# Banded attention and PReLU FFN: operands of the first layer laid out anew, and a planner that counts the order's rhythm

## The chip, the cores and the metric

The kernel runs on one core of a Trainium2 chip. The metric is the device time of one execution in microseconds (us). PE is the matmul engine (its weight loads have a row of their own, PEld), DVE the vector engine, ACT the scalar engine, POOL the GpSimd engine; SP issues the DMAs.

## The reference

Eight batches of eight heads, 576 positions, head size 64, all float32. The two parts run one after the other:

```
scores = q @ k.T / 8, kept where 0 <= i - j < 64
x = softmax(scores) @ v              # rearranged to 4608 tokens x 512
h = x @ w_in                         # 512 -> 2048
g = max(h, 0) + alpha * min(h, 0)    # alpha of each hidden column
out = g @ w_out                      # 2048 -> 512
```

## The kernel before

**Tiles and blocks.** The 4608 tokens are 36 tiles (`t`) of 128; four tiles are a block (`n`, 0 to 8). Matmuls run in fp32r: each value is a high part and a rest, and a product is hi times hi, hi times rest and rest times hi.

**First phase (to about 492 us).** Attention of a tile on PE is scores (`s.t`, line 548, 32 matmuls), then softmax on DVE, ACT and POOL, then the turning of the weights, then the values (`av`, line 604, one `av` for two tiles). A tile is turned either by PE (`tu.t`, line 588, 8 transposes; tiles listed in `PE_TURNED`, and ACT or DVE copies the result) or by DVE (`turn_by_vector`, lines 581 and 583, 16 transposes of 32x32 blocks). Blocks 0 and 1 take x through the first layer in cells (`h`, line 789, 12 matmuls of 512 columns; 16 cells a block). Blocks 2 to 8 use Strassen-like forms: a block has four groups (`d`), and a group has seven products (`p.n.d.i`, line 823) of 12 matmuls of 256 columns, in the order i = 1, 6, 5, 2, 7, 3, 4. Product 7 adds to a bank that DVE has combined from products 1, 6 and 5 (line 844). After the last products come PReLU on ACT and DVE (lines 837, 838) and a store of g to DRAM.

**Second phase (from about 492 us).** g is fetched again and made into seven forms a group (lines 934, 939, 940), which lie in ten slots used in turn (`yh_0` to `yh_9`); 252 products of 12 matmuls (`O`, line 967) follow, and the sums of the banks (line 975) and the writes of out.

**Order.** All instructions are written out in an order that `Program.order` plans: it knows a cost and a due time (`key`) for each step, and at each moment each engine takes the ready step that is due first. On PE products and attention steps compete by their keys. A group's product number `at` is due at `base + at * QUARTERS`; groups are `4 * CELL2` = 13.68 apart. Scores and values are due 0.03 ahead of the first product of a group, one score a group and one `av` every second group; the turning by PE falls due between the fifth and the sixth product. `convert_out` makes the weights of the second phase in four portions, one in each of the blocks 2, 4, 6 and 7 (`CONVERT_AT`).

**Addresses.** In a group's product the weights are the stationary operand and x the moving one. All weights lie at the same place modulo 512 bytes. From the sizes of the tiles (`step` 128 bytes, a row of x of 4160 bytes, gaps of 128 and 192 bytes) the distance from weights to x, modulo 256 bytes, is 128 for the products 1, 7 and 3 and 192 for 6, 5, 2 and 4 (5 and 6 read the buffers `s_forms`, sh and sl in the profile). In the cells of blocks 0 and 1 half of the matmuls have 128, half 192. In the second phase the forms are stationary and the weights move. Slots 0 to 3, 8 and 9 lie at 64 or 192 of the same count. Slots 4 to 7 can be shifted by steps of 64 bytes: usually by one step (64 or 192 again), but in the turns of the ring in `LEADS` (eight of them) slots 4, 5, 6 and 7 are shifted by 0, 1, 2 and 3 steps:

```
SHIFTS = [(x - 4, x - 4) if 4 <= x < 8 and turn in LEADS else (1, 1) for turn in range(26) for x in range(10)]
```

Of the kernel before, what the change touches and what calls it, by code (L numbers as in the profile page):

```python
# [23 lines left out]
BEGIN = 20.0  # L24
# [3 lines left out]
QUARTERS = 1.39  # L28
SINGLE = (0.5, 0.5, 9.5, 12.5, 28.0, 33.0, 35.0, 38.5)
HALVES = (11.0, 18.0)  # L30
EARLY_HALVES = 3
PACE = 3.8000000000000003
FIRST_TURN = 61.5
REBIASED = (0, 4, 5, 6, 8, 11, 12, 13, 14, 15)
PE_TURNED = (8, 14, 15, 17, 18, 19, 21, 22, 23, 25, 27, 28, 30, 31, 33, 34, 35)
CONVERT_AT = {2: 0, 4: 1, 6: 2, 7: 3}
# [5 lines left out]
CELL2 = 3.42  # L42
# [8 lines left out]
LEADS = (0, 1, 2, 3, 5, 8, 12, 17)  # L51
# [17 lines left out]
class Program:  # L69
# [25 lines left out]
    def order(self, fill):  # L95
# [10 lines left out]
        left, filling, warm_at = len(ops), False, None  # L106

# [38 lines left out]
        while left:  # L146
            for e in ENGINES:
# [17 lines left out]
                if e == "PE":  # L165
                    warm_at = now + COLD if warm_at is None else warm_at
                    o.busy *= 1 + (now < warm_at)
                if e == "POOL" and o.busy or e == "DVE" and o.paired:
                    o.busy += max(0.0, shared - now)
                    shared = now + o.busy  # L170
# [67 lines left out]
def banded_attention_then_prelu_ffn(  # L238
# [49 lines left out]
    def chunk_of(part, a):  # L288
        y, x = divmod(a, 2)
        return part[:, y, x * BT * P:(x + 1) * BT * P]  # L290

    def chunks_of(part, x, tiles):

        return part[:, :, x * BT * P:(x + 1) * BT * P].rearrange("p a (i q) -> p i a q", q=P)[:, tiles]

    def quarter_of(part, y, m):
        return part[:, y, :2 * BT * P].rearrange("p (x t) -> p x t", x=2)[:, :, m * 2 * P:(m + 1) * 2 * P]

    xs = [buffers_of_x(const, 0)]
# [6 lines left out]
    const.tile([P, 16], F32, name="rest")  # L306
# [359 lines left out]
    def quarter_parts(ts):  # L666

        n = ts[0] // BT
        for x in range(2):
            a21, a22 = (bank_of(V_BANK[x]).rearrange("p (i a) q -> p a i q", i=2)[:, a] for a in range(2))  # L670
            k = halves_of(V_BANK[x])
            hi, lo = (chunks_of(part, x, slice(2, BT))[:, :, 1] for part in xs[n % 2])
# [7 lines left out]
    def x_form(n, i):  # L680
# [4 lines left out]
        elif i in (5, 6):  # L685
# [3 lines left out]
        return ([quarter_of(part, y, m) for part in xs[slot]],  # L689
# [22 lines left out]
    def x_parts(ts, by=V_BANK):  # L712
# [4 lines left out]
        pieces = [([x], [chunks_of(part, x, slice(i, i + len(ts))) for part in xs[n % 2]],  # L717
# [27 lines left out]
    def attend_two(ts, begin, pace, before):  # L745
# [27 lines left out]
    def cell(n, f, key, m=None):  # L773
# [12 lines left out]
        def emit():  # L786
            for k, (w, v) in enumerate(((w_hi, xh), (w_hi, xl), (w_lo, xh))):
                for a in range(NP):
                    nc.tensor.matmul(h, w[KEPT + f][:, a * P:(a + 1) * P], chunk_of(v, a)[:, half], start=k == a == 0, stop=k == 2 and a == NP - 1, skip_group_check=True)
# [17 lines left out]
    def group(n, d, base):  # L807
# [6 lines left out]
        def product(at, i, bank, new):  # L814
# [3 lines left out]
            def emit():  # L818
# [46 lines left out]
    SHIFTS = [(x - 4, x - 4) if 4 <= x < 8 and turn in LEADS else (1, 1) for turn in range(26) for x in range(10)]  # L865
# [51 lines left out]
    def second(n):  # L917
# [4 lines left out]
        for d in range(DUOS):  # L922
# [10 lines left out]
            def both(name, to, a, b, op, reads, writes):  # L933
                add(name, "DVE", 0.61, lambda: nc.vector.tensor_tensor(out=to(), in0=a(), in1=b(), op=op), reads, writes)  # L934

            def parts(i, value, ks):
# [4 lines left out]
                    [*ks, *his], los)  # L941
# [64 lines left out]
    for n in range(NB):  # L1006
        step, off = (CELL, 0.5) if n < N0 else (CELL2, 0.01)
# [86 lines left out]
```

## Time and profile before

| | |
|---|---|
| three runs, us | median 846.36 (845.23 to 850.14) |
| profiled execution, us | 847.71 |
| its span, first to last instruction, us | 846.0 |
| granted TensorE clock, mean | 1.000 |
| PE, DVE, ACT, POOL busy, share of the span | 98%, 81%, 61%, 44% |

A profile shows one execution. Matmuls are pipelined: the busy time of one is longer than the time to the start of the next, so what a product takes is read from the starts of instructions in the timeline. There a line stands for several like instructions in a row ("x2"), and a product of 12 matmuls is six such lines, of which the rows below show the first. In the second phase a line holds four matmuls and a product three lines.

### The profile page before, as it was taken

The page shows a single profiled execution, that of the slowest core. Times are in us where ns is not written, and L with a number is a line of the kernel's source. Part 1 is how long each engine was busy: PE and PEld are TensorE (multiplying, and loading weights), DVE is VectorE, ACT ScalarE, POOL GpSimd, SP SyncE. Part 2 cuts the span into 40 slices and gives each one's busy share as a digit, 9 for nine tenths or more (in the row PEclk, how much of TensorE's full clock was granted, in tenths as well). Part 3 has the DMA queues.
Part 4 walks back from the last instruction along what each step waited for, and adds up shares of the span by engine and source line. Part 5 has one row for each costly group of instructions (what it writes and reads, how often), then busy time and mean ns, then how long its engine had stood idle before and what let it go on. Part 6 is the DMA issues. An engine that isn't in the chain of part 4 may idle for free.

```text
span 846.0 us, 23601 instructions
## 1 busy us (share of the span) xinstructions
PE 832.5 (98%) x8998; PEld 798.2 (94%) x8998; DVE 688.3 (81%) x1773; ACT 513.9 (61%) x1388; POOL 374.9 (44%) x368
## 2 busy tenths in 40 slices
PE   8999999999999999999999989999999999999998
PEld 8987788999999999999999989999999999999998
DVE  4888897879888888888875599979797887969794
ACT  6887757777778775697865664444443444444441
POOL 5899899989564661738557862000000000000000
PEclk9999999999999999999999999999999999999999
DMA  8886456445766743676574893537262543526341
GB/s 248 273 271 190 152 171 203 150 149 180 250 238 202 229 169 127 222 240 208 176 234 156 280 307 109 156 106 219 63 207 79 172 131 119 158 102 198 103 140 50
DMA packets 108880, 150.95 MB, mean 178 GB/s; under 512 B 10464, under 2 KB 69856, under 8 KB 108768
## 3 DMA queue, kind: packets, MB, share of 16 engines
q1 hardware_dynamic: 106416, 149.19, 55.1%
q8 instruction: 70, 1.15, 0.6%
q10 hardware_dynamic: 2352, 0.27, 0.2%
q14 instruction: 42, 0.34, 0.1%
HBM read 94.90 MB, written 54.53 MB: 177 GB/s over the span
## 4 chain that ended last, share of the span: by engine, by line
PE 68%; DVE 6%; ACT 2%; issue 2%; DMA 2%; SPq 0%; DVEq 0%; ACTq 0%
PE bank L967 39%; PE bank L823 24%; PE bank L604 2%; PE bank L548 2%; DVE cell L838 1%; DVE yl L940 1%; PE bank L588 1%; DVE bank L844 1%; DMA wo<-val 1%; ACT cell L837 1%; DVE g L934 1%; DMA raw<-w_out 1%; ACT r L851 0%; ACT w L564 0%; DVE pt L581 0%
## 5 line engine op out<-in xcount | busy, mean ns | idle before, releaser
L940 DVE TENSOR_TENSOR yl<-g,yh 128x512 fp32r<-128x512 f32 x216 | 149.5, 712 | 39.5 <-ACT yh L939 36.4
L939 ACT CAST yh<-g 128x512 fp32r<-128x512 f32 x216 | 125.1, 619 | 92.4 <-DVE g L934 64.9
L967 PE MATMUL bank<-wh,yl 128*128 128x256 f32 x1008 | 156.5, 277 | 2.4 <-DVE yl L940 2.3
L967 PE MATMUL bank<-wh,yh 128*128 128x256 f32 x1008 | 156.1, 277 | 1.0 <-DVE cell L838 1.0
L967 PE MATMUL bank<-wl,yh 128*128 128x256 f32 x1008 | 155.9, 277 | 0.0
L967 PEld LDWEIGHTS bank<-wh,yl 128*128 128x128 f32 x1008 | 133.6, 188 | 3.2 <-DVE yl L940 3.2
L967 PEld LDWEIGHTS bank<-wh,yh 128*128 128x128 f32 x1008 | 133.6, 188 | 1.2 <-DVE cell L838 1.2
L967 PEld LDWEIGHTS bank<-wl,yh 128*128 128x128 f32 x1008 | 133.6, 188 | 0.0
L564 ACT ACTIVATE w<-w,nm 128x128 f32<-128x128 f32 x288 | 112.4, 394 | 23.5 <-DVE nm L557 23.3
L838 DVE SCALAR_TENSOR_TENSOR cell<-bank,alphas,cell 128x256 f32<-128x256 f32 x224 | 96.0, 478 | 33.0 <-ACT cell L837 31.8
L823 PE MATMUL bank<-xh,wh 128*128 128x256 f32 x560 | 116.5, 290 | 3.8 <-DVE bank L844 2.4
L837 ACT ACTIVATE cell<-bank,alphas 128x256 f32<-128x256 f32 x224 | 91.5, 473 | 43.4 <-DVE bank L844 21.3
L823 PE MATMUL bank<-xl,wh 128*128 128x256 f32 x560 | 111.1, 280 | 0.0
L823 PE MATMUL bank<-xh,wl 128*128 128x256 f32 x560 | 111.0, 280 | 0.0
L573 POOL TENSOR_TENSOR w<-w,rc 128x512 f32<-128x512 f32 x72 | 76.1, 1074 | 53.3 <-DVE rc L569 39.9
L823 PEld LDWEIGHTS bank<-xh,wh 128*128 128x128 f32 x560 | 85.0, 188 | 10.0 <-DVE bank L844 4.8
L823 PEld LDWEIGHTS bank<-xh,wl 128*128 128x128 f32 x560 | 85.5, 188 | 0.0
L823 PEld LDWEIGHTS bank<-xl,wh 128*128 128x128 f32 x560 | 85.4, 188 | 0.0
L934 DVE TENSOR_TENSOR g<-g,g 128x512 f32<-128x512 f32 x108 | 77.0, 713 | 0.7
L844 DVE TENSOR_TENSOR bank<-bank,r 128x512 f32<-128x512 f32 x84 | 58.4, 695 | 23.2 <-PE bank L823 10.2
L557 DVE CUSTOM_DVE_ANT_0 w<-bank,masks 128x128 f32<-128x128 f32 x288 | 64.8, 285 | 10.3 <-PE bank L548 10.0
L939 ACT CAST yh<-diff 128x512 fp32r<-128x512 f32 x36 | 22.4, 623 | 76.3 <-DVE diff L934 56.2
(96 smaller groups left out, 1499.2 us busy)
## 6 DMA issues: line engine op xcount, KB each, us to landing
g<-g SPq DMA_DIRECT2D x144, 256.0 KB, 4.6
g<-cell SPq DMA_DIRECT2D x141, 256.0 KB, 3.1
out<-cell SPq DMA_DIRECT2D x36, 256.0 KB, 2.4
q<-qT SPq DMA_DIRECT2D x35, 256.0 KB, 4.3
raw<-w_out SPq DMA_DIRECT2D x16, 512.0 KB, 5.4
wl<-wo SPq DMA_DIRECT2D x28, 256.0 KB, 4.4
v<-vN SPq DMA_DIRECT2D x18, 384.0 KB, 5.3
k<-kT SPq DMA_DIRECT2D x17, 384.0 KB, 4.3
```

What stands on the lines that cost most here:

```text
L548: nc.tensor.matmul(bank_of(score_banks(t, a)[x])[us, 2 * a + h], q[r, a, h, us], kring[r, a, at + u:at + u + 2, h, :], start=True, stop=True)
L557: nc.vector.tensor_tensor_reduce(out=of_head(weights[t % 2], g), in0=bank_of(score_banks(t, g // NP)[x])[:, e].rearrange("p (b k) -> p b k ...
L564: nc.scalar.activation(w, w, AF.Exp, scale=-1.0, bias=least[t % 2][:, g:g + 1], accum_out=sums[:, t % 2, g, 0:1])
L573: nc.gpsimd.tensor_tensor(out=w, in0=w, in1=rc.unsqueeze(1).unsqueeze(3).broadcast_to(list(w.shape)), op=ALU.mult)
L823: nc.tensor.matmul(h, at_place(w, place)[:, c * P:(c + 1) * P], v[:, c], start=new and j == 0 and not done, stop=j == 1 and done == 5, ski ...
L837: add(f"sl.{n}.{d}.{m}.{x}.{j}", "ACT", 0.36, lambda h=h, g=g, f=f: nc.scalar.activation(g, h, AF.Copy, scale=slope[:, f:f + 1]), ["signs" ...
L838: add(f"la.{n}.{d}.{m}.{x}.{j}", "DVE", 0.43, lambda h=h, g=g, f=f: nc.vector.scalar_tensor_tensor(out=g, in0=h, scalar=sign[:, f:f + 1], ...
L844: add(f"{name}.{n}.{d}", "DVE", 0.6, lambda: nc.vector.tensor_tensor(out=to, in0=a, in1=b, op=ALU.add), reads, k_to)
L934: add(name, "DVE", 0.61, lambda: nc.vector.tensor_tensor(out=to(), in0=a(), in1=b(), op=op), reads, writes)
L939: add(f"ys.{u}.{i}.h", "ACT", 0.54, lambda: nc.scalar.copy(y_of(y_hi, x, hi), value()), [*ks, "right"], his)
L940: add(f"ys.{u}.{i}.l", "DVE", 0.61, lambda: nc.vector.tensor_tensor(out=y_of(y_lo, x, lo), in0=value(), in1=y_of(y_hi, x, hi).bitcast(F32) ...
L967: nc.tensor.matmul(banks[bank][:, h * EH:(h + 1) * EH], part[:, j * HW + h * P:j * HW + (h + 1) * P], w[k][:, j * EH:(j + 1) * EH], start= ...
```

## The change

It has these parts.

- **Layout of x.** The buffers of x lose their gaps, so that all lie 192 bytes from the weights (modulo 256). `s_forms` now holds products 5 and 7 in place of 5 and 6, and product 7's buffers stand after a gap that puts them at 128. So of the seven products only 7, the fifth of the order, lies at 128. The cells of blocks 0 and 1 are all at 192.
- **Due times.** Products are due every 1.362 (`STEP`); the sixth and seventh are due at the same time as the fifth (`VISIT`). Groups are 12.72 apart (`CELL2` = 3.18). Attention in blocks 2 to 8 is due 7 products earlier (`EARLIER`), and the turning by PE a whole group, or two, after the tile's pair begins (`TURNS`), so that all attention steps of a group are due 3.13 to 3.16 after its first product.
- **Costs in the planner.** A product costs 1.425 if it is a 7, 1.362 if only products have run since a 7, else 1.413; a change between products and anything else on PE costs 0.1. DVE passes of the second phase are counted as sharing a port with POOL (`paired`).
- **Tiles and portions.** Tiles 15, 19 and 23 are turned by DVE, no longer by PE. The first two portions of `convert_out` move from blocks 2 and 4 to 3 and 5. The starts of blocks 0 and 1 are shifted by 0.5 to 4.5.
- **Lead-in.** In the turns of `LEADS` (eight again, other ones) only slot 6 is shifted, by two steps, which is 128; the other slots stay at one step.

```diff
-BEGIN = 20.0
+BEGIN = 23.0
-QUARTERS = 1.39
-SINGLE = (0.5, 0.5, 9.5, 12.5, 28.0, 33.0, 35.0, 38.5)
-HALVES = (11.0, 18.0)
+SLOW, ENTRY, CHANGE = 1.413, 1.425, 0.1
+TURNS = (1.0, 2.0)
+HOLD = 0
+VISIT = 4.0
+EARLIER = 7.0
+SINGLE = (0.5, 0.5, 9.5, 11.5, 28.0, 30.5, 35.5, 37.5)
+HALVES = (12.0, 18.0)
-FIRST_TURN = 61.5
+FIRST_TURN = 57.0
-PE_TURNED = (8, 14, 15, 17, 18, 19, 21, 22, 23, 25, 27, 28, 30, 31, 33, 34, 35)
-CONVERT_AT = {2: 0, 4: 1, 6: 2, 7: 3}
+PE_TURNED = (8, 14, 17, 18, 21, 22, 25, 27, 28, 30, 31, 33, 34, 35)
+CONVERT_AT = {3: 0, 5: 1, 6: 2, 7: 3}
-CELL2 = 3.42
+CELL2 = 3.18
-LEADS = (0, 1, 2, 3, 5, 8, 12, 17)
+LEADS = (0, 1, 2, 3, 4, 5, 7, 9)
...
+        steady, lately = False, ("", 0.0)
...
+                if e == "PE":
+                    quarters, before = o.name[:2] == "p.", lately[0][:2] == "p."
+                    if quarters:
+                        steady = steady and before and now - lately[1] < 0.05
+                        entry = o.name[-1] == "7"
+                        o.busy = ENTRY if entry else STEP if steady else SLOW
+                        steady = steady or entry
+                    o.busy += CHANGE * (quarters != before)
+                    lately = o.name, now + o.busy
...
-    const.tile([P, 32], F32, name="step")
-
-    def buffers_of_x(pool, slot):
-
-        both = []
-        for x in "hl":
-            both.append(pool.tile([P, 2, 2 * BT * P + 16], F32R, name=f"x{x}_{slot}"))
-            if x == "h":
-                pool.tile([P, 32], F32, name=f"gap_{slot}")
-        return both
...
-    xs = [buffers_of_x(const, 0)]
+    const.tile([P, 48], F32, name="step")
+    xs = [[const.tile([P, NP, BT * P], F32R, name=f"x{x}_0") for x in "hl"]]
...
-    const.tile([P, 16], F32, name="rest")
+    const.tile([P, 48], F32, name="rest")
...
-    xs.append(buffers_of_x(odd, 1))
+    xs.append([odd.tile([P, NP, BT * P], F32R, name=f"x{x}_1") for x in "hl"])
+    s_forms = {5: [odd.tile([P, 2, 2 * P], F32R, name=f"s{x}_5") for x in "hl"]}
     odd.tile([P, 48], F32, name="gap")
-    s_forms = {i: [odd.tile([P, 2, 2 * P], F32R, name=f"s{x}_{i}") for x in "hl"] for i in (5, 6)}
+    s_forms[7] = [odd.tile([P, 2, 2 * P], F32R, name=f"s{x}_7") for x in "hl"]
...
-                turned_by_pe(t, V_BANK, begin + (0.5 + i) * pace)
+                turned_by_pe(t, V_BANK, begin + (TURNS[i] if t // BT >= N0 else 0.5 + i) * pace - 0.02)
...
-            add(f"p.{n}.{d}.{i}", "PE", QUARTERS, emit, [k for x in "hl" for place in places for k in w_keys_of(x, place[0], [place[1]])] + ks[0] + ks[1],
-                halves_of(bank), key=base + at * QUARTERS)
+            add(f"p.{n}.{d}.{i}", "PE", STEP, emit, [k for x in "hl" for place in places for k in w_keys_of(x, place[0], [place[1]])] + ks[0] + ks[1],
+                halves_of(bank), key=base + (at * STEP if at < 5 else VISIT * STEP - HOLD))
...
-    SHIFTS = [(x - 4, x - 4) if 4 <= x < 8 and turn in LEADS else (1, 1) for turn in range(26) for x in range(10)]
+    SHIFTS = [(2, 2) if x == 6 and turn in LEADS else (1, 1) for turn in range(26) for x in range(10)]
...
-        step, off = (CELL, 0.5) if n < N0 else (CELL2, 0.01)
+        step, off = (CELL, 0.5) if n < N0 else (CELL2, 0.01 + EARLIER * STEP / CELL2)
```

The rest of the diff adapts the views of x to its new layout and adds `paired=True` to the DVE passes of lines 934 and 940.

## Rows read from the trace of the kernel before

**Rows 1.** The page: busy time of each engine (part 1), the chain's lines (part 4).

```profile
PE 832.5 (98%) x8998; PEld 798.2 (94%) x8998; DVE 688.3 (81%) x1773; ACT 513.9 (61%) x1388; POOL 374.9 (44%) x368
...
PE bank L967 39%; PE bank L823 24%; PE bank L604 2%; PE bank L548 2%; DVE cell L838 1%; DVE yl L940 1%; PE bank L588 1%; DVE bank L844 1%; DMA wo<-val 1%; ACT cell L837 1%; DVE g L934 1%; DMA raw<-w_out 1%; ACT r L851 0%; ACT w L564 0%; DVE pt L581 0%
```

**Rows 2.** Windows: us, busy (instructions) PE PEld DVE ACT POOL, PEclk, DMA share, GB/s.

```profile
147.00:399.00 252.00, 249.79 (x3359) 241.81 (x3355) 213.78 (x731) 189.94 (x612) 164.03 (x158) 1.00 0.60 195
348.00:399.00 51.00, 50.52 (x697) 48.42 (x696) 44.82 (x153) 39.81 (x125) 31.36 (x27) 1.00 0.67 216
399.00:451.00 52.00, 51.45 (x615) 50.08 (x614) 39.19 (x108) 36.07 (x98) 33.92 (x30) 1.00 0.58 193
...
492.00:530.00 38.00, 34.64 (x290) 33.65 (x289) 37.58 (x48) 19.44 (x37) 16.89 (x11) 1.00 0.54 176
```

**Rows 3.** Timeline of PE, 238 to 251 us: start, us, what, xcount.

```profile
241.15 0.39 PE L823 MATMUL bank<-sh,wh 128*128 128x256 f32 x2
...
242.51 0.39 PE L823 MATMUL bank<-xh,wh 128*128 128x256 f32 x2
...
243.97 1.10 PE L548 MATMUL bank<-k,q 64*64 64x128 f32 x32
245.00 0.50 PE L823 MATMUL bank<-xh,wh 128*128 128x256 f32 x2
...
246.53 0.40 PE L823 MATMUL bank<-xh,wh 128*128 128x256 f32 x2
...
247.95 0.40 PE L823 MATMUL bank<-xh,wh 128*128 128x256 f32 x2
...
249.34 0.40 PE L823 MATMUL bank<-xh,wh 128*128 128x256 f32 x2
...
250.77 0.40 PE L823 MATMUL bank<-sh,wh 128*128 128x256 f32 x2
```

**Rows 4.** Timeline of PE, 366 to 372 us.

```profile
368.37 0.40 PE L823 MATMUL bank<-sh,wh 128*128 128x256 f32 x2
...
369.78 0.40 PE L823 MATMUL bank<-xh,wh 128*128 128x256 f32 x2
...
371.20 1.03 PE L588 MATMUL bank<-ident,w 128*128 128x128 f32 x8
371.99 0.37 PE L823 MATMUL bank<-xh,wh 128*128 128x256 f32 x1
```

**Rows 5.** Timeline of PE: the first and the last attention visit of the 49.

```profile
159.26 1.10 PE L548 MATMUL bank<-k,q 64*64 64x128 f32 x32
...
438.96 2.04 PE L604 MATMUL bank<-pt,v 64*64 64x128 f32 x96
```

**Rows 6.** Groups by line on DVE, 147 to 451 us: the 32x32 transposes.

```profile
L581 DVE STREAM_TRANSPOSE pt<-w 32x256 f32<-32x256 f32 x56 | 24.4, 435 | 1.5 <-POOL w L573 0.4
L583 DVE STREAM_TRANSPOSE pt<-w 32x128 f32<-32x128 f32 x56 | 17.0, 303 | 1.2
```

**Rows 7.** Waits, 147.04 to 492.25 us: us in total, times, longest.

```profile
PE bank L823 <- DVE bank L844: 2.4, 4, 1.0
...
PE bank L823 <- DVE cell L838: 1.0, 3, 0.5
```

**Rows 8.** Timeline of PE, 542 to 552 us, second phase.

```profile
544.15 0.64 PE L967 MATMUL bank<-wh,yh 128*128 128x256 f32 x4
...
547.00 0.64 PE L967 MATMUL bank<-wh,yh 128*128 128x256 f32 x4
...
548.43 0.63 PE L967 MATMUL bank<-wh,yh 128*128 128x256 f32 x4
...
549.84 0.62 PE L967 MATMUL bank<-wh,yh 128*128 128x256 f32 x4
```

**Rows 9.** Timeline of PE, 99 to 106 us: matmuls of 512 columns.

```profile
99.68 1.09 PE L789 MATMUL bank<-xh,wh 128*128 128x512 f32 x4
...
102.46 1.09 PE L789 MATMUL bank<-xh,wh 128*128 128x512 f32 x4
```

More of the change, by code (lines that the diff above doesn't have):

```diff
@@ L276, in banded_attention_then_prelu_ffn @@
     w_hi, w_lo = ([const.tile([P, 512], F32R, name=f"w{x}_{k}") for k in range(7 * DUOS)] for x in "hl")
-    const.tile([P, 32], F32, name="step")
-    def buffers_of_x(pool, slot):
-        both = []
-        for x in "hl":
-            both.append(pool.tile([P, 2, 2 * BT * P + 16], F32R, name=f"x{x}_{slot}"))
-            if x == "h":
-                pool.tile([P, 32], F32, name=f"gap_{slot}")
-        return both
[L288 to L297, printed above, removed]
-    xs = [buffers_of_x(const, 0)]
+    const.tile([P, 48], F32, name="step")
+    xs = [[const.tile([P, NP, BT * P], F32R, name=f"x{x}_0") for x in "hl"]]
     sums_of = [const.tile([P, 512], F32, name="r_0")]
@@ L671, in quarter_parts @@
             k = halves_of(V_BANK[x])
-            hi, lo = (chunks_of(part, x, slice(2, BT))[:, :, 1] for part in xs[n % 2])
+            hi, lo = (part.rearrange("p (a x) (i q) -> p x i a q", x=2, q=P)[:, x, 2:, 1] for part in xs[n % 2])
             his, los = (x_keys(part, 4 * (n % 2) + 2 + x, range(2, 4)) for part in ("xh", "xl"))
@@ L684, in x_form @@
             (y, m), slot = rows[i], n % 2
-        elif i in (5, 6):
+        elif i in s_forms:
             return s_forms[i], [[f"s{x}.{i}"] for x in "hl"]
@@ L688, in x_form @@
             (y, m), slot = (0, 1), (N0 + (i == 3)) % 2
-        return ([quarter_of(part, y, m) for part in xs[slot]],
+        return ([part[:, 2 * y:2 * y + 2, m * 2 * P:(m + 1) * 2 * P] for part in xs[slot]],
                 [[k for c in (2 * y, 2 * y + 1) for k in x_keys(part, 4 * slot + c, (2 * m, 2 * m + 1))] for part in ("xh", "xl")])
@@ L716, in x_parts @@
         copy, other, pass_ = (0.48, 0.6, 0.61) if len(ts) == 2 else (0.36, 0.34, 0.35)
-        pieces = [([x], [chunks_of(part, x, slice(i, i + len(ts))) for part in xs[n % 2]],
+        pieces = [([x], [part.rearrange("p (a x) (i q) -> p x i a q", x=2, q=P)[:, x, i:i + len(ts)] for part in xs[n % 2]],
                    bank_of(by[x]).rearrange("p (i a) q -> p i a q", i=2)[:, :len(ts)], halves_of(by[x])) for x in range(2)]
@@ L788, in emit @@
                 for a in range(NP):
-                    nc.tensor.matmul(h, w[KEPT + f][:, a * P:(a + 1) * P], chunk_of(v, a)[:, half], start=k == a == 0, stop=k == 2 and a == NP - 1, skip_group_check=True)
+                    nc.tensor.matmul(h, w[KEPT + f][:, a * P:(a + 1) * P], v[:, a, half], start=k == a == 0, stop=k == 2 and a == NP - 1, skip_group_check=True)
         tiles = range(BT) if m is None else range(m * BT // 2, (m + 1) * BT // 2)
@@ L933, in both @@
             def both(name, to, a, b, op, reads, writes):
-                add(name, "DVE", 0.61, lambda: nc.vector.tensor_tensor(out=to(), in0=a(), in1=b(), op=op), reads, writes)
+                add(name, "DVE", 0.61, lambda: nc.vector.tensor_tensor(out=to(), in0=a(), in1=b(), op=op), reads, writes, paired=True)
             def parts(i, value, ks):
@@ L940, in parts @@
                 add(f"ys.{u}.{i}.l", "DVE", 0.61, lambda: nc.vector.tensor_tensor(out=y_of(y_lo, x, lo), in0=value(), in1=y_of(y_hi, x, hi).bitcast(F32), op=ALU.subtract),
-                    [*ks, *his], los)
+                    [*ks, *his], los, paired=True)
             a11, a12, a21, a22 = (cell(q) for q in range(4))
@@ L1041, in banded_attention_then_prelu_ffn @@
     add("right", "POOL", 0.0, open_right, (), [*early_keys, "right"])
-    add("left", "POOL", 0.0, open_left, ["right"], [*odd_x, *staged[0], *staged[1], *(f"s{x}.{i}" for x in "hl" for i in (5, 6)), "left"])
+    add("left", "POOL", 0.0, open_left, ["right"], [*odd_x, *staged[0], *staged[1], *(f"s{x}.{i}" for x in "hl" for i in s_forms), "left"])
     for n in range(NB):
```

## Prediction

> **What bounds the kernel now.** I read the page first [rows 1]: PE is busy 98% of the span, and the chain that ended last lies for 39% on the products of the second phase and for 24% on those of the groups. DVE is next, at 81%. Then the windows, to see whether another engine is close in a stage [rows 2]. While groups and attention run together (147 to 451 us, two rows of the group) PE is all but always busy, and DVE has 213.78 + 39.19 = 253.0 of 304 us, 83%; its densest block is 348 to 399 with 44.82 of 51, 88%. Only between the phases, 492 to 530, does DVE fill its time (37.58 of 38) and PE stand still for some 3.4 us. So the first phase is as long as PE's list of work, and since a busy PE is not one at its peak, the question is how long each product takes from its start to the next start. That is what the timeline of PE shows.
>
> In [rows 3] the reader sees products 5 and 2 of a group, a visit of attention (scores), 7, 3, 4 and the next group's 1, with a product from the s buffers behind it. The starts are apart by 1.36 (5), 1.46 (2, with scores behind it), 1.03 (the scores), 1.53 (7, with scores ahead of it), 1.42 (3), 1.39 (4), 1.43 (1). Three prices follow. A product at distance 128 takes 1.42 to 1.43; I use 1.425. The first at 192 behind one at 128 takes 1.39, every further one 1.36. And a visit costs 0.10 on the product ahead of it and 0.10 on the one behind it. A fourth price is in [rows 4]: two products at 192 that follow a visit with no product at 128 between take 1.41 each. So a quick rhythm is entered by way of a product at 128, kept by products at 192, and lost at 128 and at many visits.
>
> **Rhythm of the products.** There are 28 groups (7 blocks of 4). Over 7 x 1.36, a group now spends 3 x 0.065 on 1, 7 and 3 and 2 x 0.03 on the products behind them: 0.255, in all 7.1 us. Afterwards only 7 is at 128: 0.065 + 0.03 = 0.095 a group, 2.7 us. By the keys attention comes 3.13 to 3.16 after a group's first product, between the third (due 2.72) and the fourth (4.09); so in the 24 groups with attention I expect a visit ahead of product 2, which then runs at 1.41: 24 x 0.05 = 1.2. If attention in fact falls ahead of 7, this is 0. I take 3.9 in place of 7.1: **-3.2** (bounds -4.4, and +3.2 if the quick rhythm isn't entered, below).
>
> **Visits.** In the timeline of 147 to 492 I count 49 visits, of which [rows 5] has the first and the last; 28 begin with scores or values, which make the product ahead of them longer, while one that begins with transposes costs it 0.01 (1.42 after 1.41 in [rows 4]). With one due time a group, a pair of tiles needs in its first group the turning of its first tile and the next pair's scores together, and in the second the scores and values, in one visit, or in two where the second tile is turned by PE (the values wait for the copies of its turned weights; meanwhile product 2 runs). With 7 such pairs and 4 others, 7 x 3 + 4 x 2 and one more at the start: 30 visits, some 18 of them with a price ahead. That saves 19 x 0.10 + 10 x 0.09: **-2.8** (bounds 0 and -4, the latter with a visit in each of the 24 groups).
>
> **Turning.** Three tiles fewer on PE, at 0.79 for eight transposes [rows 4]: **-2.4**. In exchange DVE gets 8 x 0.435 + 8 x 0.303 = 5.9 us a tile [rows 6], 17.7 us in all, and loses at most some copies of turned weights. This is hidden only while DVE has slack: 253.0 + 17.7 = 270.7 us in what would be 296 us is 91%, above the 88% of its densest block. Behind a late DVE stand the sums of line 844 that product 7 waits for, the PReLU passes that free a bank, and the next scores' minima. PE now waits 2.4 + 1.0 us for DVE there [rows 7], 1.0 of it in one wait. I let half of the 2.4 come once more: **+1.2** (bounds 0, as PE's visits give the sums more time, and +12, below).
>
> **Lead-in.** Of the second phase's slots 4 to 7, four products in a turn of `LEADS` take 549.84 - 544.15 = 5.69, which is 0.25 over 4 x 1.36; eight turns, 2.0 us [rows 8]. Slot 6, at 128, takes 1.43 there and the next 1.41. Afterwards only these two remain, 0.07 + 0.03 to 0.05, eight times 0.11: 0.9 us. **-1.1** (bounds -1.3 and 0, if leaving out slots 4 and 5 keeps the rhythm from returning).
>
> **What I cost at nothing.** The cells of blocks 0 and 1: 12 matmuls of 512 columns take 2.78 [rows 9]; at the quick rate of two products they would take 2.72, at 1.41 2.82, so with 29 whole cells the bounds are -1.7 and +1.2. The other starts of blocks 0 and 1 shift steps of a PE that has no idle time in that stage: -2 to +2. Between the phases the plan now knows that DVE and POOL share a port, which can reorder the forms and weights; PE's idle time of 3.4 us there bounds this: -3.4 to +3.4. The portions of `convert_out` that move, with 4 loads and 7 stores each on SP's queue, feed only the second phase, over 200 us later; the DMA engines are at 0.60 in 147 to 399 [rows 2], so there is room. The DVE work of those portions stays the same in sum. The layout adds no instruction.
>
> **Sum.** -3.2 - 2.8 - 2.4 + 1.2 - 1.1 = -8.3. The span of 846.0 becomes 837.7, and with the 1.7 that the profiled execution has outside it 839.4 in place of 847.7. That execution was 1.35 above the median of the three, 846.36, so the forecast of the median is 838.0 us.
>
> A rule of the Trainium skill speaks against the largest terms. TensorE: Matmul & The Clock Gate, section "Step-by-step: what each phase is for", says that TensorE reads weights and moving operand through two independent ports, so that loading the next weights takes no read bandwidth from the running matmul. Read strictly, where the operands lie would not matter, and of the sum only visits and turning would be left (the second rival). The trace disagrees: products of the same shape, back to back, take 1.36 or 1.43.
>
> **Rivals.** (1) *The quick rhythm isn't entered behind 7.* Then the six products at 192 stay at 1.41: 0.065 + 6 x 0.05 = 0.365 a group, 10.2 us against 7.1 now, +3.1 in place of -3.2: 844.3. For it: [rows 4], where the rhythm once lost stayed lost, and 7 now has a visit close ahead. Against: 4 behind 3 in [rows 3]. Chance 0.13.
> (2) *Addresses aren't the cause*, the two paces come from something that travels with the products' order: rhythm and lead-in give nothing, -2.8 - 2.4 + 1.2 = -4.0: 842.4. The rule of the Trainium skill named above would have it so. Against: the second phase, where the only thing that differs in the turns of `LEADS` is the shift [rows 8]. Chance 0.05.
> (3) *DVE becomes the bound*, the case on the other side. If it can't be filled beyond the 88% of its best block, 270.7 us of work need 308 us where PE would need 296: +12, 849.6. At the mean of 147 to 399, 213.78 / 252 = 85%, they need 319 us: 861. It decides at 89%: there the gain is gone. For it: DVE works in a fixed order and often stands behind ACT. Against: those waits shrink when DVE is the late one, and in 492 to 530 it was filled to 99% [rows 2]. Chance 0.12.
> (4) *More is won*: attention ahead of 7 (-1.2), cells at the quick rate (-1.7), half of the idle time between the phases (-1.7): 833.4. Chance 0.15.
>
> My forecast keeps 0.55. A change of 0.5%, 4.2 us, is about what a measurement of this kernel tells from none. Below 842.1 lie nearly all of the forecast's own cases (0.52), (4), half of (2) and a few of (1): 0.72. Above 850.6 lies about two thirds of (3) and a little else: 0.10. Between, 0.18. The range takes in (4) with the lower bounds of the small terms, 831, and (1), (2) and the near end of (3), 847; outside are the rest of (3) and several lower bounds at once.
>
> **What would show it.** Rhythm: in the timeline of a block such as the fifth, starts 1.36 apart for 4, 1, 6 and 5, and one of 1.39 behind 7; six at 1.41 would be rival 1. Visits: about 30 in the stretch of the groups, and a tu alone only ahead of product 2. Turning: 13 tiles of transposes on PE there; DVE at 90% in the windows, and PE's waits for lines 844 and 838 not far above 3.4 us; 10 us or more would be rival 3. Lead-in: in turns such as the eighth one product at 1.43, with 1.36 ahead of it. The first group should start near 147, the second phase near 485. The forecast is wrong if the scores aren't ready when due, so that visits scatter, if 7 waits for its DVE sums in most groups, or if the idle time between the phases grows by several us because the last portions and forms come no sooner than before.

## The result, and the profile after

The changed kernel takes 836.58 us (median of 4 runs, 836.05 to 837.52), the kernel before 848.25 beside it (4 runs, 845.23 to 851.24): a ratio of 0.9864, 95% interval 0.9821 to 0.9906. Over the longer series that went with the experiments the kernel before stood at 846.72 to 846.92, so the gain is 10.1 to 10.3 us rather than the 11.7 of this pair. The profiled execution of the changed kernel took 836.5 us with a span of 834.8, where before had 847.7 and 846.0: 11.2 us less span, and 8.3 were forecast.

The page of the changed kernel, busy time of each engine and the chain by line; lines 817 and 961 are what 823 and 967 were in [rows 1]:

```profile
PE 823.8 (99%) x8974; PEld 792.0 (95%) x8974; DVE 704.9 (84%) x1821; ACT 518.1 (62%) x1382; POOL 386.3 (46%) x368
...
PE bank L961 41%; PE bank L817 13%; DVE cell L832 1%; PE bank L598 1%; DVE bank L838 1%; PE bank L582 1%; DMA q<-qT 1%; PE bank L542 0%; ACT cell L831 0%; DVE w L551 0%; ACT w L558 0%; DVE pt L577 0%; DVE pt L575 0%; ACT r L845 0%; DVE xl L717 0%
```

PE's busy time fell by 8.7 us and DVE's rose by 16.6. The windows (columns as in [rows 2]) say where:

```profile
147.00:399.00 252.00, 247.48 (x3356) 239.64 (x3355) 233.70 (x790) 190.25 (x616) 168.56 (x160) 1.00 0.62 206
...
451.00:492.00 41.00, 40.15 (x343) 39.80 (x342) 30.15 (x54) 28.25 (x62) 35.53 (x28) 1.00 0.85 275
492.00:530.00 38.00, 38.00 (x331) 38.00 (x330) 33.27 (x50) 20.98 (x37) 19.41 (x8) 1.00 0.73 246
```

In 147 to 399 DVE is busy 233.70 of 252 us, 93%, where it had 85%, and PE has lost 2.3 us of busy time. In 492 to 530 PE is busy all the time, where 34.64 of 38 us were busy before. The two show the two halves of the story: the groups run with a fuller DVE, and the stretch between the phases has lost its idle time.

The timeline of PE over one group of block 4, of each product the first line (each stands for two of its twelve matmuls):

```profile
262.47 0.39 PE L817 MATMUL bank<-xh,wh 128*128 128x256 f32 x2
...
263.83 0.39 PE L817 MATMUL bank<-sh,wh 128*128 128x256 f32 x2
...
265.19 1.03 PE L582 MATMUL bank<-ident,w 128*128 128x128 f32 x8
266.16 1.10 PE L542 MATMUL bank<-k,q 64*64 64x128 f32 x32
267.19 0.50 PE L817 MATMUL bank<-xh,wh 128*128 128x256 f32 x2
...
268.68 0.40 PE L817 MATMUL bank<-sh,wh 128*128 128x256 f32 x2
...
270.11 0.40 PE L817 MATMUL bank<-xh,wh 128*128 128x256 f32 x2
...
271.50 0.39 PE L817 MATMUL bank<-xh,wh 128*128 128x256 f32 x2
...
272.86 0.39 PE L817 MATMUL bank<-xh,wh 128*128 128x256 f32 x2
```

Against [rows 3]: products 6 and 5 take 1.36 each, the turning and the scores now lie in one visit ahead of product 2, product 7 at 128 takes 1.43 (268.68 to 270.11), 3 behind it 1.39, and from 4 on it is 1.36.

**The sum by one walk.** For each kernel I walked along PE's matmuls from the first group's product to the end of the last product of the second phase. The 448 products are taken at 1.36 each, 609.28 us; what is above that is sorted by the steps from one matmul's start to the next. Steps of 113 to 119 ns are the rhythm. A first or last step of a product above 150 ns is the price of a visit; a last one above 260, or one in the middle above 150, is a wait. Two things the sorting mixes: a wait behind a visit, ahead of the next product, falls into attention's own time, and where the granted clock was at half behind a long wait (e3, e4 and e11) the slower steps, 1.4 to 2.1 us in each, fall into the waits. Columns: the stretch in us, number of visits, rhythm of the groups' products, price of visits, attention's own time (scores, values, turning), waits in the groups, waits in the second phase, and the rhythm and visits of the second phase. Each line adds up to its stretch within 0.02.

```
                     stretch visits rhythm price attention waits g waits 2nd 2nd
before                695.01   49    7.05  8.54   58.50     4.55    4.76     2.32
after                 684.16   32    4.74  6.68   55.21     6.73    0.16     1.36
e10 late fetch        690.63   32    4.08  6.70   55.21     8.53    5.78     1.04
e3 unpaired           694.52   32    4.08  6.66   55.21    10.06    7.98     1.26
e1 addresses back     684.52   32    8.23  5.99   55.03     4.48    0.16     1.34
e2 no entry           682.80   32    5.49  6.08   55.09     5.35    0.16     1.34
e5 turned by PE       691.13   35    4.64  7.20   57.69     9.06    1.82     1.43
e4 attention late     715.94   41    4.97  9.01   60.45    29.88    1.37     0.99
e6 no leads           695.61   32    3.73  6.61   55.22     7.08    0.22    13.47
e9 fourth behind      684.12   34    4.37  6.37   57.18     4.18    1.80     0.95
e8 layout alone       693.62   49    4.31  8.88   59.39     4.62    4.80     2.34
e11 before, fetch     698.29   49    7.01  8.41   58.60     5.84    6.57     2.59
e12 fetch + paired    690.92   49    6.91  8.28   58.60     3.92    1.70     2.24
e13 e2, sooner lead   684.09   32    4.83  6.50   55.08     7.24    0.27     0.90
```

Each line is one profiled execution. After, e2, e6 and e13 run the groups by the same plan and have 5.35 to 7.24 us of waits there, so less than 2 us in that column tells nothing. What lies ahead of the first group's product is left out: it was 145.8 to 148.5 us in ten of the fourteen profiles and 151.2 to 152.8 in the other four (e1, e4, e8, e11; last section).

From before to after the walk gives -2.31 in the rhythm, -1.86 in the price of visits, -3.29 in attention's time, +2.18 in the groups' waits, -4.60 in the second phase's waits, and -0.96 in its rhythm: -10.85, with -0.53 ahead of the stretch and +0.19 behind it the 11.2 of the span.

**Where the largest part came from.** Three products of the second phase now run among the last groups. The timeline of PE, first lines of the first such product and of the group's product behind it, and the fetch of g on SP's queue that it hangs on:

```profile
451.23 1.33 SPq L921 DMA_DIRECT2D g<-g  x3
```

```profile
462.28 0.63 PE L961 MATMUL bank<-wh,yh 128*128 128x256 f32 x4
...
463.69 0.41 PE L817 MATMUL bank<-sh,wh 128*128 128x256 f32 x2
```

The first fetch and the first product of the second phase in the kernel before:

```profile
480.95 1.38 SPq L927 DMA_DIRECT2D g<-g  x3
```

```profile
492.25 0.63 PE L967 MATMUL bank<-wh,yh 128*128 128x256 f32 x4
```

There the fetch came 29.7 us later, no product of the second phase ran until the last of the groups had been issued, and the first ones then stood waiting for their forms: 2.3 us for line 940 and 1.0 for line 838. The program issues the fetch of g `earliest=base - 45` ahead of the second phase as the plan dates it, and that date hangs on `CELL2`, which the change lowered from 3.42 to 3.18: 28 groups of 4 x 0.24 are 26.9 us, less the 3 by which `BEGIN` rose, so the second phase was dated 23.9 us sooner. So a constant of the groups' pace moved the fetch.

**Where it was given back.** PE's waits for lines 838 and 832 (844 and 838 before, [rows 7]), groups only; columns: us in total, times, longest:

```profile
PE bank L817 <- DVE bank L838: 4.7, 9, 0.9
PE bank L817 <- DVE cell L832: 0.6, 2, 0.5
```

5.3 us against 3.4. Six of the eleven, 3.1 us, have one form, as here in the timeline of PE in block 5: product 3, then 4.

```profile
333.64 0.39 PE L817 MATMUL bank<-xh,wh 128*128 128x256 f32 x2
...
335.63 0.50 PE L817 MATMUL bank<-xh,wh 128*128 128x256 f32 x2 [0.46 <-DVE bank L838]
```

Product 4 needs a bank that DVE adds up from what 7 left, and only 3 lies between. Along the timelines, a visit lay between 7 and 4 in 11 of the 28 groups before and lies there in none now; a visit stood right ahead of 7 in 21 groups and now stands there in 10. So DVE has less time for that sum; but in [rows 3] the three lie together too and PE doesn't wait, so the order alone doesn't make the wait. In five of the six DVE's two passes of line 832 (the PReLU) come shortly ahead of the late sum, in the one shown a pass of 1.41 us of `convert_out`.

### The profile page after: what moved, and what is told of

Its sections match the earlier page's. It is cut to its first block, busy times and chain, and to the rows that moved or that the text cites. A ratio compares the mean times of both kernels' runs of the same rounds, so it can differ in the third digit from the quotient of the medians.

```text
span 834.8 us, 23747 instructions
## 1 busy us (share of the span) xinstructions
PE 823.8 (99%) x8974; PEld 792.0 (95%) x8974; DVE 704.9 (84%) x1821; ACT 518.1 (62%) x1382; POOL 386.3 (46%) x368
## 4 chain that ended last, share of the span: by engine, by line
PE 56%; DVE 3%; ACT 1%; DMA 1%; issue 1%; DVEq 0%; ACTq 0%; SPq 0%
PE bank L961 41%; PE bank L817 13%; DVE cell L832 1%; PE bank L598 1%; DVE bank L838 1%; PE bank L582 1%; DMA q<-qT 1%; PE bank L542 0%; ACT cell L831 0%; DVE w L551 0%; ACT w L558 0%; DVE pt L577 0%; DVE pt L575 0%; ACT r L845 0%; DVE xl L717 0%
## 5 line engine op out<-in xcount | busy, mean ns | idle before, releaser
L933 ACT CAST yh<-g 128x512 fp32r<-128x512 f32 x216 | 132.8, 622 | 129.2 <-PE bank L961 85.6
L817 PE MATMUL bank<-xh,wh 128*128 128x256 f32 x560 | 113.2, 283 | 3.7 <-DVE bank L838 3.1
L551 DVE CUSTOM_DVE_ANT_0 w<-bank,masks 128x128 f32<-128x128 f32 x288 | 64.6, 284 | 10.3 <-PE bank L542 10.0
L558 ACT ACTIVATION_READ_ACCUMULATOR w<-w,nm 128x1 f32 x288 | 56.1, 195 | 0.0
```

Of the source, the lines that this page charges most:

```text
L551: nc.vector.tensor_tensor_reduce(out=of_head(weights[t % 2], g), in0=bank_of(score_banks(t, g // NP)[x])[:, e].rearrange("p (b k) -> p b k ...
L558: nc.scalar.activation(w, w, AF.Exp, scale=-1.0, bias=least[t % 2][:, g:g + 1], accum_out=sums[:, t % 2, g, 0:1])
L817: nc.tensor.matmul(h, at_place(w, place)[:, c * P:(c + 1) * P], v[:, c], start=new and j == 0 and not done, stop=j == 1 and done == 5, ski ...
L933: add(f"ys.{u}.{i}.h", "ACT", 0.54, lambda: nc.scalar.copy(y_of(y_hi, x, hi), value()), [*ks, "right"], his)
```

## The experiments

All are the changed kernel with one edit, but for three that start from the kernel before (e8, e11, e12). All compute the whole reference. Ratios are to the kernel before, with their 95% intervals.

**e10: the fetch as late as before.**

```diff
-  ..., service=0.9, earliest=base - 45)
+  ..., service=0.9, earliest=base - 21)
```

> The changed kernel with one edit: the second phase's fetches of g may start 24 us later in the plan, where the kernel before had them. Theory A (the earlier fetch, a side effect of the shorter group spacing, closed the idle time between the phases): PE's waits in the second phase return, 3 to 5 us, the median goes from 836.6 to 840 to 841.5, and no second-phase product runs before the last group product. Theory B (the DVE passes counted as sharing POOL's port closed it): within 1 us of 836.6.

842.57 us (9 runs, 841.32 to 846.69), ratio 0.9951 (0.9934 to 0.9968): 6.0 us of the gain are gone. Waits of PE, by the view of waits of the stretch 146 to 530:

```profile
PE bank L961 <- DVE yl L934: 3.7, 3, 1.7
PE bank L961 <- ACT cell L831: 0.9, 1, 0.9
```

The second phase waits for its forms again, 5.78 us in the walk against 0.16, and none of its products runs among the groups. Without the early fetch the gap stays open.

**e3: the DVE passes of the forms without their marks.**

```diff
-  ..., op=op), reads, writes, paired=True)
+  ..., op=op), reads, writes)
-  ..., [*ks, *his], los, paired=True)
+  ..., [*ks, *his], los)
```

> The changed kernel without the two marks that count DVE passes of the second phase as sharing a port with POOL. Theory A (earlier fetch): within 1 us of 836.6. Theory B (these marks closed the idle time between the phases): 3 to 5 us more, 840 to 841.5.

845.03 us (10 runs, 839.52 to 847.35), ratio 0.9971 (0.9952 to 0.9991). 8.5 us are gone, though the fetch is as early as in the changed kernel. I had expected the marks to matter little; that was wrong. The view of waits, 146 to 530:

```profile
PE bank L817 <- DVE bank L838: 7.1, 10, 2.0
...
PE bank L961 <- POOL wh L387: 3.1, 1, 3.1
```

Both the groups' sums and POOL's weights for the second phase come late. Behind that one wait of 3.1 us, which ended at 525.76, the granted clock stood near half, 1.2 GHz, from about 527 to 531. How I read it, which no run isolates: without the marks the plan takes these passes for as short beside POOL as without it, and places too much around them.

**e11 and e12: the same two on the kernel before.** First the fetch alone, then the fetch and the marks.

```diff
-  ..., service=0.9, earliest=base - 45)
+  ..., service=0.9, earliest=base - 69)
```

> The kernel before with the fetch of g allowed 24 us sooner, nothing else; its plan then puts three products of the second phase ahead of the last product of the groups, as the changed kernel's does. Theory F (the early fetch alone fills the gap between the phases): PE's waits in the second phase fall from 4.76 to below 1.5 us, time down by 3 to 5 us, to 842 to 844. Theory B (fetch and the marks of the DVE passes as sharing a port are both needed, as the runs without either suggest): the waits come back inside the last groups, the time within 1.5 us of the kernel before.

> The run before plus the two marks of DVE passes as sharing a port with POOL, all else as in the kernel before. Theory B (both are needed): 841.5 to 843.5, at least 2 us below the run with the fetch alone, PE's waits from the first O product on below 1 us. Theory F: the same as the fetch alone, within 1 us.

e11: 854.06 us (6 runs, 851.56 to 856.73), ratio 1.0072 (1.0047 to 1.0096). Part of this lies ahead of the groups (first product at 152.8), but the walk too is 3.3 us longer than before. Three products of the second phase do run among the last groups, as in the changed kernel, but the groups' waits rise by 1.3 us, which tells nothing, and those of the second phase from 4.76 to 6.57. The longest of them in the timeline of PE:

```profile
534.08 0.74 PE L967 MATMUL bank<-wh,yh 128*128 128x256 f32 x4 [2.87 <-POOL wh L393]
```

That is the wait of e3 once more, with the granted clock near half behind it from about 535 to 539. PE waits for POOL's weights in the second phase of e3 and e11 alone, the two runs with the early fetch and without the marks.

e12: 844.44 us (10 runs, 844.08 to 849.09), ratio 0.9976 (0.996 to 0.9992), a little above the 841.5 to 843.5 of theory B, the walk 4.1 us below before. Neither theory had the fetch alone slower. That the two work only together is shown from both sides now: e10 and e3 take one away from the changed kernel, and e11 and e12 add first one and then both to the kernel before.

**e1: the addresses of before in the changed kernel.** Buffers of x, their views, the gaps and the s buffers as before; the plan goes on believing in the new rhythm.

```diff
-    const.tile([P, 48], F32, name="step")
-    xs = [[const.tile([P, NP, BT * P], F32R, name=f"x{x}_0") for x in "hl"]]
+    const.tile([P, 32], F32, name="step")
+    xs = [buffers_of_x(const, 0)]
...
-    s_forms[7] = [odd.tile([P, 2, 2 * P], F32R, name=f"s{x}_7") for x in "hl"]
+    s_forms = {i: [odd.tile([P, 2, 2 * P], F32R, name=f"s{x}_{i}") for x in "hl"] for i in (5, 6)}
```

> The changed kernel with the layout of x of the kernel before: products 1, 7 and 3 at 128, order and due times kept as changed. Theory R (the distance sets the pace): products 1 and 3 take 1.42, 4 and 6 behind them 1.39, so the excess of the group products over 1.36 goes from 4.7 to about 8, and the cells lose their 0.02: +2.5 us, 839. Rival (addresses aren't the cause): within 0.5 us of 836.6, the same starts.

838.75 us (4 runs, 836.07 to 841.57), ratio 0.9901 (0.9874 to 0.9929). In the walk the rhythm costs 8.23 in place of 4.74, the 3.5 us that the addresses should be worth; but the groups' waits are 4.48 in place of 6.73, and the price of visits 5.99 in place of 6.68. The stretch is only 0.4 us longer. The median is 2.2 us higher; but of the four executions the two with a granted clock of 1.000 took 836.07 and 837.86, about what the changed kernel takes, and the two with 0.995 and 0.997 took 841.57, the profiled one, and 839.63. In the profiled one the first group's product came 4.7 us later (last section). That the waits took back the gain rests on one profiled execution, and 2.25 us is little more than the spread of one plan.

**e8: the addresses alone, on the kernel before.** The reverse edit; plan, visits and turned tiles as before.

> The kernel before with the new layout of x alone: of a group's products only 7 lies at 128 in place of 1, 7 and 3; the plan, its due times, the lead-ins and the turned tiles stay as they were. Theory R (the distance to the operand sets the pace, and DVE's sums take part of the gain back): the product excess over 1.36 falls from 7.05 to 4 to 5 us; visits stay 49; PE's waits for DVE grow by 0.5 to 2 us; the time falls by 1 to 2.5 us, to 844.3 to 845.8. Theory N (the gain of the rhythm needs the other parts of the change): excess of products as before, 6.5 or more, and the time within 0.5 us of the kernel before.

847.03 us (10 runs, 844.53 to 850.99), ratio 0.9994 (0.9971 to 1.0017): nothing that can be told. The rhythm falls from 7.05 to 4.31, as it should; the stretch falls by only 1.4, since attention's blocks take 0.9 longer (the transposes, 14.85 against 14.01, with 0.5 of it in waits for DVE behind them) and visits 0.3 more: half of what the products save is spent in other places on PE.

**e2: no product at 128 at all.** The gap is moved behind the s buffer of 7, so all seven lie at 192.

```diff
-    odd.tile([P, 48], F32, name="gap")
     s_forms[7] = [odd.tile([P, 2, 2 * P], F32R, name=f"s{x}_7") for x in "hl"]
+    odd.tile([P, 48], F32, name="gap")
```

> The changed kernel with the 192-byte gap moved behind the buffers of product 7, so that all seven products are at 192. Theory R (the quick rhythm, once lost at a visit, is entered again by a product at 128): the products after a visit stay at 1.41 until the next wait or visit lets them in; 7 itself takes 1.41 or 1.36 in place of 1.425; in all +1 to +4 us, 837.5 to 840.5, with runs of 5 and more products at 1.41 in the timeline. Rival (the more products at 192 the better, no entry is needed): -1.8 us, 834.8.

836.06 us (4 runs, 835.61 to 837.24), ratio 0.9871 (0.9854 to 0.9887), no different from the changed kernel. Of 75 products in e2 that follow one at 1.41 directly, 6 became quick, four of them behind a wait. In the changed kernel 2 of the 22 that follow one at 192 and 1.41 became quick, but 25 of the 28 that follow product 7: the product at 128 is a way in, as the forecast had it. It isn't the only one: with no product at 128 in the groups 11 of 32 products behind a visit are quick in e2. So the entry is worth only 0.75 us of rhythm (5.49 against 4.74), as its own 1.425 in 28 groups has to be paid.

**e5: three tiles turned by PE again.**

```diff
-PE_TURNED = (8, 14, 17, 18, 21, 22, 25, ...
+PE_TURNED = (8, 14, 15, 17, 18, 19, 21, 22, 23, 25, ...
```

> The changed kernel with tiles 15, 19 and 23 turned by PE again: 17.7 us of DVE work less, 2.4 to 2.8 us of PE work more and 3 more visits. Theory D (DVE is nearly the bound while attention runs, so PE's waits for it take back part of what its products save): the waits of the group products fall from 6.7 to 4 or below, and the median stays within 1.5 us of 836.6. Theory P (PE alone is the bound; the waits have other causes): the waits stay above 6, and the median is 3 us more, 839.5.

844.13 us (10 runs, 842.53 to 848.32), ratio 0.9959 (0.9936 to 0.9982). Both theories missed: the time is 7.5 us above the changed kernel's, not 1.5 or 3. The turning is +2.5 as costed, and DVE is back at 212.14 us in 147 to 399. PE's waits, first from 146 to 451 us, then from 451 to 492:

```profile
PE bank L817 <- DVE bank L838: 2.8, 7, 0.7
PE bank L817 <- DVE cell L832: 0.3, 1, 0.3
```

```profile
PE bank L817 <- DVE bank L838: 3.7, 4, 2.2
```

Up to 451 the waits fell, to 3.1 from the changed kernel's 4.5 (3.9 + 0.6 in the same stretch), so a less full DVE does help there. Behind 451 they are 3.7, the longest 2.2 at 469, and the second phase waits 1.8. The longest is no backlog of DVE, which had itself stood waiting for the product just ahead:

```profile
467.02 0.70 DVE L838 TENSOR_TENSOR bank<-bank,r 128x512 f32<-128x512 f32 x1 [2.49 <-PE bank L817]
```

A copy by ACT and a second sum had to follow before PE could go on. Why a plan with three tiles more for PE has less room there I have not isolated: each such edit makes the planner order that block anew.

**e4: attention as late in the group as before**, with the other constants of the change.

```diff
-TURNS = (1.0, 2.0)
+TURNS = (0.5, 1.5)
-EARLIER = 7.0
+EARLIER = 0.0
```

> The changed kernel with the due times of attention of the kernel before (right ahead of a group's first product, the turning half a group later). Theory V (fewer visits save 0.2 us each): 41 visits in place of 32, +1.5 to +2 us of ramps; DVE's sums for product 7 are no longer covered by a visit, so the waits grow by 1 to 4 us too: 839 to 842. Rival (only the number of products matters): within 0.7 us of 836.6.

869.81 us (4 runs, 866.0 to 873.78), ratio 1.0264 (1.0212 to 1.0316): far more than either theory gave for it. The windows, and the waits of 146 to 530:

```profile
147.00:399.00 252.00, 230.62 (x3039) 217.89 (x3037) 224.78 (x733) 176.18 (x559) 154.67 (x142) 1.00 0.56 181
```

```profile
PE bank L817 <- DVE bank L838: 18.0, 16, 4.6
PE bank L817 <- DVE cell L832: 3.8, 3, 1.5
```

and one of those waits in the timeline of PE, product 2 and behind it product 7:

```profile
242.51 0.40 PE L817 MATMUL bank<-xh,wh 128*128 128x256 f32 x2
...
244.98 0.51 PE L817 MATMUL bank<-sh,wh 128*128 128x256 f32 x2 [0.89 <-DVE bank L838]
```

DVE is busy 89% of that window, less than the 93% of the changed kernel, and PE stands still for 21.4 of 252 us against 4.5. So how full DVE is on average doesn't decide. In the wait shown DVE did four transposes, 1.79 us, and then the sum that 7 needs. My reading is that a visit gives such a sum its time: 17 of the 18.0 us stand at products 7, 3 and 4 with no visit right ahead of them. It is not shown. The changed kernel has no visit ahead of 3 or 4 in any group and loses 3.1 us there, the kernel before has attention due as late as e4 and waits 4.55 us in its groups, and the edit has the planner order DVE's work anew as well. Also, 4.6 of the 18.0 are one wait, at 488 among the forms of the second phase, with the granted clock near half behind it from about 487 to 494.

**e9: product 4 due behind the next group's 1.**

```diff
-  ... else VISIT * STEP - HOLD))
+  ... else VISIT * STEP - HOLD if at < 6 else 4 * CELL2 + 0.01))
```

> The changed kernel with product 4 due just behind the next group's product 1, so that one product more lies between 7 and 4, which waits for DVE's sum of 7. Theory W (the waits of 0.6 to 1.0 us ahead of 4 are a matter of order): the waits of the group products fall from 6.7 to 3 or below, -2 to -4 us, 833 to 834.5. Theory D (DVE is nearly the bound, so the waits turn up elsewhere): within 1 us of 836.6.

838.23 us (4 runs, 835.62 to 838.57), ratio 0.9884 (0.9847 to 0.9921). The groups' waits fall by 2.5 us, attention's blocks grow by 2.0, most of it waits for DVE behind a visit (1.9 us against 0.5), and the second phase waits 1.6 more; the stretch is the same, 684.12. Waits for DVE that are chased from one place turned up in another here, with DVE busy 233.42 of the 252 us.

**e6: no lead-ins.**

```diff
-LEADS = (0, 1, 2, 3, 4, 5, 7, 9)
+LEADS = ()
```

> The changed kernel with no slot shifted to 128 in the second phase. Theory R (once lost, the quick rhythm comes back by way of 128 alone as long as PE has no wait): the second phase keeps 1.41 from its first products to its end, some 235 products by 0.053, +12 us, 849. Rival (it comes back by itself within some tens of products): -0.3 to +2 us.

Ten executions: 834.83, 835.62 and 836.73 us, and seven of 846.35 to 852.43. The profiled one took 848.1. Its timeline of PE near the end, first lines of two products, and the same place in the changed kernel:

```profile
822.29 0.63 PE L961 MATMUL bank<-wh,yh 128*128 128x256 f32 x4
...
823.70 0.63 PE L961 MATMUL bank<-wh,yh 128*128 128x256 f32 x4
...
825.11 0.64 PE L961 MATMUL bank<-wh,yh 128*128 128x256 f32 x4
```

```profile
820.99 0.62 PE L961 MATMUL bank<-wh,yh 128*128 128x256 f32 x4
...
822.35 0.62 PE L961 MATMUL bank<-wh,yh 128*128 128x256 f32 x4
...
823.71 0.62 PE L961 MATMUL bank<-wh,yh 128*128 128x256 f32 x4
```

1.41 against 1.36, kept to the end: 13.47 us in the walk against 1.36. The lead-ins are worth 12 us where the rhythm doesn't come by itself, and by the times alone nothing in the three executions in which it seems to.

**e13: e2 with one lead-in more, ahead of the first turn.** In the changed kernel the second phase ran at 1.41 until the lead-in at 510.47:

```profile
509.05 0.63 PE L961 MATMUL bank<-wh,yh 128*128 128x256 f32 x4
...
510.47 0.64 PE L961 MATMUL bank<-wh,yh 128*128 128x256 f32 x4
...
511.89 0.63 PE L961 MATMUL bank<-wh,yh 128*128 128x256 f32 x4
...
513.27 0.62 PE L961 MATMUL bank<-wh,yh 128*128 128x256 f32 x4
```

```diff
-    SHIFTS = [(2, 2) if x == 6 and turn in LEADS else (1, 1) ...
+    SHIFTS = [(2, 2) if x == 6 and turn in LEADS or x == 7 and turn == 0 else (1, 1) ...
```

> The changed kernel with all seven x operands at 192 (as the run without entry) and one lead-in more: slot 7 of the first turn also lies at 128, so the second phase should be quick from its second product on. Theory R: second-phase excess 0.6 to 0.9 in place of 1.36, span 0.5 to 0.8 below the run without entry, 835.2 to 835.8. Rival: the rhythm comes no sooner by one product at 128, since the products of the second phase only became quick at 510 us in the changed kernel: 836 to 836.6.

837.0 us (4 runs, 833.99 to 839.63), ratio 0.9875 (0.9837 to 0.9912). The second phase's 1.34 became 0.90, as forecast; it is lost in the groups' waits of the profiled execution (7.24) and in the spread of the four runs. No version beat the changed kernel by more than can be told.

## Why the prediction was right, step by step

The forecast was 838.0 us for 836.6, and the sum -8.3 for a span that fell by 11.2. The sign and most of the terms held; one term that was costed at nothing was the largest of all. The walk's counterparts of the five terms of the sum come to -6.2, two us short of it, and the 4.6 that nobody had counted made up for that and more: that the time came out within 1.4 us owes something to luck.

- **Rhythm, -3.2: measured -2.3.** The mechanism held: 1.36 for the products at 192, 1.43 for 7, 1.39 behind it, the entry by way of 128 (e2), and +3.5 when the addresses are put back (e1). The size is a little off because products behind a visit often stay at 1.41. But this term doesn't come through: alone on the kernel before it gives 1.4 us of walk and no time that can be told (e8), and taken out of the changed kernel it leaves the stretch 0.4 us longer. The forecast added the terms as if each were free of the others. In e1 the waits for DVE and the visits gave back most of the rhythm, in e8 the transposes and visits half of it.
- **Visits, -2.8: measured -1.9**, with 32 visits where I counted on 30; 19 stood ahead of product 2, where I expected them all, and 10 ahead of 7. When attention falls due was taken for a matter of 0.10 a visit. e4 shows that it is worth some 20 us: 29.88 us of waits in the groups against 6.73, 2.0 of them steps at half the clock.
- **Turning, -2.4: measured -2.7** on line 582, with 0.6 less on the values. DVE's side came as costed, in groups by line on DVE, 147 to 451:

```profile
L575 DVE STREAM_TRANSPOSE pt<-w 32x256 f32<-32x256 f32 x73 | 31.8, 435 | 1.4 <-POOL w L567 0.2
L577 DVE STREAM_TRANSPOSE pt<-w 32x128 f32<-32x128 f32 x80 | 24.2, 303 | 1.6
```

80 where there were 56 [rows 6], at the same 435 and 303 ns (7 records of the first line are missing from the trace); DVE's 233.70 + 35.94 = 269.6 us in 147 to 451 against the 270.7 worked out.
- **Waits for DVE, +1.2: measured +2.2** in the walk, +1.9 in the view of waits. The forecast looked for them at product 7; 3.1 us came at 4, behind 7 and 3, and 1.7 at 7.
- **Lead-in, -1.1: measured -0.9 to -1.0.**
- **The step that failed: the idle time between the phases, costed at nothing with bounds of -3.4 to +3.4.** It gave -4.6. The bound was too small, since it was read from PE's idle time in 492 to 530, and the walk, which counts the slow steps at a restart too, has 4.76 for the second phase before. The forecast saw the marks of lines 928 and 934 and named them, but overlooked that `CELL2` dates the fetch of g; e10, e3, e11 and e12 show that it takes the two together and that one alone doesn't close the gap.
- **The cells of blocks 0 and 1** take 2.80 at line 783 where line 789 took 2.78 [rows 9], +0.02 on each of 29: they did not enter the quick rhythm with all of them at 192. The first group's product came at 146.5, near the 147 forecast.

Of the rivals, the one on the other side (DVE as the bound, deciding at 89%) is refuted as it was put: DVE went to 93%, and PE's waits grew by 2 us. Waits for DVE can be large all the same, as e4 shows at 89%. "The quick rhythm isn't entered behind 7" can be seen in e2, where it costs 0.75 us and not 6, since about half of its products are quick without it (93 of 196 are not). "Addresses aren't the cause" is refuted by e1 and e8 as to the rhythm (8.23 and 4.74 us, 7.05 and 4.31); as to the time it came close, for another reason. The rule of the Trainium skill that was weighed there (TensorE: Matmul & The Clock Gate, section "Step-by-step: what each phase is for", two independent read ports), read as strictly as the forecast read it, is not borne out by these two pairs. What in the chip makes the distance matter no run shows.

## What to carry to other kernels

Before a constant of a planner's pace is costed at nothing, look up every date that is worked out from it: here one that stood for the length of a group also dated a fetch of the next phase, and that, together with the marks on DVE's passes, was the largest part of the gain. Don't add up savings on a full engine as if each were free: of the 3.5 us that the addresses were worth on PE's products, 0.4 us was left in e1's stretch, and of the 2.7 in e8, 1.4. And the mean fullness of a second engine doesn't tell how long the first will wait for it: here PE waited far more with DVE at 89% than with DVE at 93%, by the order of the work alone.

## What the runs showed of the hardware that was not expected

The pace of a product has a memory. In the profile of e6 all 252 products of the second phase took 1.41, though they lie as the quick ones of the changed kernel do, and three of ten executions of the same program were 9.6 us or more shorter than the others. What sets the rhythm in those three isn't shown: the profiled execution was none of them.

A late first load costs more than its delay. In the profiles of e1, e4, e8 and e11 PE ran dry for 2.5 to 4.1 us near 12 us, and the granted clock then fell to half, 1.2 GHz, for some 3.5 to 7 us. In e13 PE ran dry for 2.9 us there and the clock stayed. Windows of e11, then of the changed kernel:

```profile
12.00:14.00 2.00, 0.00 (x0) 0.00 (x0) 1.10 (x9) 0.49 (x2) 0.13 (x1) 0.76 0.73 221
14.00:16.00 2.00, 1.04 (x5) 1.04 (x6) 1.97 (x19) 1.45 (x7) 1.91 (x2) 0.50 0.66 172
16.00:18.00 2.00, 2.00 (x11) 2.00 (x10) 1.93 (x5) 2.00 (x11) 0.98 (x1) 0.50 1.02 353
```

```profile
12.00:14.00 2.00, 2.00 (x20) 2.00 (x20) 1.40 (x9) 2.00 (x11) 0.78 (x1) 1.00 1.08 388
14.00:16.00 2.00, 2.00 (x25) 1.88 (x27) 1.62 (x4) 1.90 (x6) 1.30 (x2) 1.00 0.85 298
16.00:18.00 2.00, 2.00 (x58) 1.93 (x55) 0.98 (x3) 1.79 (x4) 1.44 (x2) 1.00 0.20 49
```

The first group's product then comes at 151.2 to 152.8 us in place of 145.8 to 148.5. The load is the small one of alpha, issued at 1.7 us. It landed at 7.4 us in the changed kernel and 9.1 in the kernel before, but between 11.2 and 12.5 in the four, and the first softmax stands behind it on DVE, here in e11:

```profile
12.52 0.17 DVE L380 TENSOR_SCALAR alphas<-alphas 128x16 f32<-128x16 f32 x1 [4.24 <-DMA alphas<-alpha]
```

Why it landed later there isn't shown. It fits the spread of the medians: of the 58 executions of the kernel before in the three longer series, the 51 with a mean granted clock of 0.999 or more took 845.26 to 849.14 us, the seven with less 850.35 to 852.54. Whether the clock fell at this place in those seven no profile shows.
